# More Strassen pairs in the first layer, an accumulation seeded in PSUM, and a literal instruction order for groups 2 to 8

## Chip, cores, metric

One core of one Trainium2 chip. The metric is the device time of one execution in microseconds (us). Each time given is the median of several runs (3 to 11); all were in the fast state, so nothing has to be set aside as slow.

## The reference

Linear attention, whose output goes as tokens into a SwiGLU feed-forward block:

```
q_p, k_p = phi(q), phi(k)          # phi(x) = (x if x > 0 else exp(x) - 1) + 1; B=8, H=8, S=576, D=64
kv  = einsum('bhsd,bhse->bhde', k_p, v);   z = sum(k_p over s)
att = einsum('bhsd,bhde->bhse', q_p, kv) / (einsum('bhsd,bhd->bhs', q_p, z) + 1e-6)
x   = att as (4608 tokens, 512)
out = (silu(x @ w_gate) * (x @ w_val)) @ w_out      # hidden size 1536
```

The work goes in nine groups (0 to 8) of 512 tokens. For each group the kernel needs:

- the attention products. I call J the key-value products of one batch (72 small matmuls of 64x64 array tiles) and M the products that give a group's x (8 to 16 small matmuls);
- layer 1: gate and value products for twelve blocks of 128 hidden features. Plainly, a pair of blocks is sixteen matmuls with 512 columns; as one Strassen level it is seven products of four matmuls with 256 columns;
- layer 2: seven Strassen products for each of two token halves, 256 columns each. Both kernels have this from group 2 on.

TensorE makes the products, ScalarE the exponentials, silus, casts and part of the PSUM copies, VectorE the rest.

## The kernel before

The buffers of k, v, raw q and phi(q) were all double; batch b used half b % 2:

```
k16 = two([P, HL, J * D], FP16, "k16");  q16 = two(...);  v16 = two(...)
kp  = two([P, J, HL * D], FP16, "kp");   qp  = two(...);  vm  = two(...)

def load(src, dst, b):
    nc.gpsimd.dma_start(out=dst[b % 2][:, :, :], in_=heads(src, b))
```

A Strassen pair in layer 1 (only in the last two groups, `TS = (NG - 2, NG - 1)`, five pairs each): product 1 is copied to SBUF, product 2 is made in another bank, VectorE adds the two, ScalarE takes the silu.

```
def sp_keep(p, i, from_z, scale=1.0):
    nc.scalar.activation(out=sp_bufs(p)[0][i], in_=halves(sbanks[p % 3][from_z]), func=AF.Copy, bias=0.0, scale=scale)

def sp_gadd(p, th):
    (s, gg, _, _) = sp_bufs(p)
    nc.vector.tensor_tensor(out=gg[:, th, :, :], in0=halves(sbanks[p % 3][1]), in1=s[th], op=ALU.add)

def sp_silu(p, th):
    (_, gg, sl, _) = sp_bufs(p)
    nc.scalar.activation(out=sl[:, th, :, :], in_=gg[:, th, :, :], func=AF.Silu, bias=0.0, scale=1.0)
```

The group loop places the side work by hand, after a feature block of layer 1 or a product of layer 2. M and J stand side by side (cut):

```
for g in range(1, NG):
    b1, b2, b3 = g + 1, g + 2, g + 3
    ...
    for fb in range(FB if g in TS else 0, FB):
        l1(g, fb)
        for f in sl[fb]:
            f()
        if fb == 5 and b3 < B:
            ld_b(b3)                                              # k, q, v of a batch, in this order
    ...
    for (i, step) in enumerate(l2_steps(g)):
        ...
        if i == (7 if g in TS else 12 if b2 < B else 8) and b1 < NG:
            mm2(b1, (pV[1], pG[1], pV[0], pG[0]), "AVAV")         # M; x copies: ScalarE, VectorE in turn
        ...
        if i == 12 and b2 < B:
            joint(b2)                                             # J, its R copies and z diagonals
```

Of the kernel before, what the change touches and what calls it, by code (L numbers as in the profile page):

```python
# [13 lines left out]
P = 128  # L14
# [3 lines left out]
def kernel(  # L18
# [40 lines left out]
    prod = sb.tile([P, 4, HL * D], FP16, name="prod")  # L59
# [11 lines left out]
    xT = [two([P, U * C], FP16, f"xT{i}") for i in range(4)]  # L71
# [12 lines left out]
    id16 = sb.tile([P, P], FP16, name="id16")  # L84
    idx = sb.tile([P, P], mybir.dt.int32, name="idx")
# [7 lines left out]

    def load(src, dst, b):
        nc.gpsimd.dma_start(out=dst[b % 2][:, :, :], in_=heads(src, b))  # L95
# [22 lines left out]
    def exp_(src, e, b, lp):  # L118
        s = slice(2 * lp, 2 * lp + 2)
        nc.scalar.activation(out=e[:, s, :], in_=src[b % 2][:, s, :], func=AF.Exp, bias=0.0, scale=1.0)  # L120

    def plus_1(src, dst, b, lp):
        nc.vector.tensor_scalar(
            out=dst[b % 2][:, :, P * lp:P * lp + P].rearrange("p j (s d) -> p s j d", d=D),
            in0=src[b % 2][:, 2 * lp:2 * lp + 2, :].rearrange("p s (j d) -> p s j d", d=D), scalar1=0.0, scalar2=1.0,
            op0=ALU.max, op1=ALU.add)

    def least(e, dst, b, lp):
        d = dst[b % 2][:, :, P * lp:P * lp + P].rearrange("p j (s d) -> p s j d", d=D)
        nc.vector.tensor_tensor(out=d, in0=d, in1=e.rearrange("p s (j d) -> p s j d", d=D), op=ALU.min)  # L130
# [18 lines left out]
    def vcast(b, lp):  # L149
        s = slice(2 * lp, 2 * lp + 2)  # L150
        nc.scalar.activation(out=vm[b % 2][:, :, s, 0:D].rearrange("p j l d -> p l j d"),  # L151
                             in_=v16[b % 2][:, s, :].rearrange("p l (j d) -> p l j d", d=D),
                             func=AF.Copy, bias=0.0, scale=1.0)
# [4 lines left out]
    def terms_k(b, lp):  # L158

        return (kp[1], kp[0]) if b == 0 else (kp[b % 2],)  # L160

    def mm1(b, lp):
        if lp == 0:
            kvb[b] = ((pV[2], pX[0]), (pX[2], pV[2]), (pX[0], pX[1]), (pV[0], pG[0]), (pX[2], pV[2]))[min(b, 4)]
        for j in range(J):
            for (t, term_) in enumerate(terms_k(b, lp)):
                for hh in range(2):
# [7 lines left out]
                    for e in range(2):  # L175
# [4 lines left out]
                            rhs=v16[b][rows, 2 * lp + e, D * j:D * j + D] if b < 2 else vm[b % 2][rows, j, 2 * lp + e, :],  # L180
                            start=(j == 0), stop=(j == J - 1))

    def zdiag(b, lp):
        for hh in range(2):
            nc.vector.tensor_scalar(out=zd[:, 2 * hh + lp, :], in0=id16[:, :],
                                    scalar1=kvb[b][hh][:, 256 * lp + D:256 * lp + D + 1],
                                    scalar2=1.0 / SC, op0=ALU.mult, op1=ALU.mult)

    def r_copies(b):
        W = D  # L190
        for hh in range(2):
            nc.scalar.activation(out=R[b % 2][:, hh:4:2, 0:W],
                                 in_=kvb[b][hh][:, :].rearrange("p (i c) -> p i c", i=2)[:, :, 0:W], func=AF.Copy,
                                 bias=0.0, scale=1.0)
# [16 lines left out]
    def zb_copy(b):  # L211
        for hh in range(2):
            rows = slice(C * hh, C * hh + C)
            nc.scalar.activation(out=zbc[rows, :], in_=zps[b][rows, 256 * hh:256 * hh + 256], func=AF.Copy,
                                 bias=0.0, scale=1.0)
# [38 lines left out]
    def corners(ps, lhs, b, j0, j1, lps=(0, 1)):  # L254

        for lp in lps:
            for hh in range(2):
                for e in range(2):
                    rows = slice(D * e, D * e + D)
                    nc.tensor.matmul(out=ps[2 * lp + e][C * hh:C * hh + C, :], lhsT=lhs(2 * lp + hh, e),  # L260
                                     rhs=qT[b % 2][rows, j0:j1, lp, C * hh:C * hh + C], start=True, stop=True)

    def mm2(g, ps, engs):
        us = units(g)
        c00 = 2 * C if g == 2 else 0
        for b in sorted(set(u[0] for u in us)):
            js = [j for (bb, j) in us if bb == b]
            c0 = C * us.index((b, js[0]))
            if b > 1:
                corners([x[:, c0:c0 + C * len(js)] for x in ps], kv(b), b, js[0], js[-1] + 1)  # L270
        for i in range(4):
            dst = xT[i][g % 2][:, c00:]
            if engs[i] == "A":
                nc.scalar.activation(out=dst, in_=ps[i][:, c00:], func=AF.Copy, bias=0.0, scale=1.0 / SC)
            else:
                nc.vector.tensor_scalar(out=dst, in0=ps[i][:, c00:], scalar1=1.0 / SC, scalar2=None, op0=ALU.mult)  # L276
# [25 lines left out]
    TS = (NG - 2, NG - 1)  # L302
    HN = U * C // 2
    sbanks = ((pG[0], pV[0]), (pG[1], pV[1]), (pX[2], pV[2]))

    def flat(t):
        return t[:, :, :].rearrange("p a b -> p (a b)")

    wr = rr[:, :, :].rearrange("p a b -> p (a b)").bitcast(FP16)
    wl_all = ((wr[:, 0:10 * P], wr[:, 10 * P:20 * P]), (wl2[:, 0, :], wl2[:, 1, :]), (flat(k16[0]), flat(q16[0])),  # L310
              (flat(v16[0]), flat(kp[0])))

    def wl(m, c, f0, f1):
        return wl_all[m][c][:, P * f0:P * f1]

    def wl_sum(m, c, f0, f1):
        (g1, g2, v1, v2) = [w[:, i, P * f0:P * f1] for (w, i) in ((wg, c), (wg, 2 + c), (wv, c), (wv, 2 + c))]
        (a, b, op) = ((v1, v2, ALU.add), (wl(0, c, f0, f1), g1, ALU.subtract), (g1, v1, ALU.subtract),
                      (g2, wl(1, c, f0, f1), ALU.subtract))[m]
        nc.vector.tensor_tensor(out=wl(m, c, f0, f1), in0=a, in1=b, op=op)  # L320

    def x_blk(g, kh, th, c):
        return xT[2 * kh + c][g % 2][:, HN * th:HN * th + HN]

    def x_sum(g, m, c):
        (a, b) = ((x_blk(g, 0, 1, c), x_blk(g, 0, 0, c)), (x_blk(g, 1, 1, c), xs[:, 0, c, :]),
                  (x_blk(g, 1, 1, c), x_blk(g, 0, 1, c)), (x_blk(g, 1, 0, c), xs[:, 1, c, :]))[m]
        nc.vector.tensor_tensor(out=xs[:, m, c, :], in0=a, in1=b, op=ALU.subtract)

    def sp_prd(g, p, n):  # L330
        dst = sbanks[p % 3][1 if n in (2, 3, 5) else 0]
        for e in range(2):
            for c in range(2):
                fs = slice(P * (2 * p + e), P * (2 * p + e) + P)
                lhs = {1: wg[:, c, fs], 2: wg[:, 2 + c, fs], 4: wv[:, 2 + c, fs]}
                lhs = lhs[n] if n in lhs else wl({3: 3, 5: 0, 6: 1, 7: 2}[n], c, 2 * p + e, 2 * p + e + 1)
                rhs = {1: x_blk(g, 0, 0, c), 2: x_blk(g, 1, 0, c), 3: x_blk(g, 1, 1, c), 4: xs[:, 3, c, :],
                       5: xs[:, 0, c, :], 6: xs[:, 1, c, :], 7: xs[:, 2, c, :]}[n]
                nc.tensor.matmul(out=dst[:, HN * e:HN * e + HN], lhsT=lhs, rhs=rhs,  # L339
                                 start=(n in (1, 2, 5) and e == 0 and c == 0), stop=(c == 1), skip_group_check=True)  # L340
# [4 lines left out]
    def f32(t, n):  # L345
        return flat(t).bitcast(FP32)[:, 0:n]

    def sp_bufs(p):
        i = p % 2
        s12 = f32((k16, v16)[i][1], 4 * HN).rearrange("p (i e t) -> p i e t", i=2, e=2)  # L350
        s5 = f32(q16[1], 4 * HN)[:, 2 * HN * i:2 * HN * i + 2 * HN].rearrange("p (e t) -> p e t", e=2)
        gg = f32((kp[1], ek)[i], 4 * HN).rearrange("p (h e t) -> p h e t", h=2, e=2)
        sl = vm[i][:, :, :, :].rearrange("p j l d -> p (j l d)")[:, 0:4 * HN].rearrange("p (h e t) -> p h e t", h=2, e=2)
        v22 = flat(prod)[:, 2 * HN * i:2 * HN * i + 2 * HN].rearrange("p (e t) -> p e t", e=2)
        return (s12[:, 0, :, :], s12[:, 1, :, :], s5), gg, sl, v22

    def sp_keep(p, i, from_z, scale=1.0):
        nc.scalar.activation(out=sp_bufs(p)[0][i], in_=halves(sbanks[p % 3][from_z]), func=AF.Copy, bias=0.0, scale=scale)

    def sp_gadd(p, th):  # L360
        (s, gg, _, _) = sp_bufs(p)
        nc.vector.tensor_tensor(out=gg[:, th, :, :], in0=halves(sbanks[p % 3][1]), in1=s[th], op=ALU.add)

    def sp_silu(p, th):
        (_, gg, sl, _) = sp_bufs(p)
        nc.scalar.activation(out=sl[:, th, :, :], in_=gg[:, th, :, :], func=AF.Silu, bias=0.0, scale=1.0)  # L366

    def sp_v22(p):
        (s, _, _, v22) = sp_bufs(p)
        nc.vector.scalar_tensor_tensor(out=v22, in0=halves(sbanks[p % 3][0]), scalar=SC, in1=s[2], op0=ALU.mult, op1=ALU.add)  # L370

    def sp_h21(g, p):
        nc.vector.scalar_tensor_tensor(out=hT[g % 2][:, 2 * p:2 * p + 2, 0:HN], in0=halves(sbanks[p % 3][0]), scalar=SC,
                                       in1=sp_bufs(p)[2][:, 0, :, :], op0=ALU.mult, op1=ALU.mult)

    def sp_h22(g, p):
        (_, _, sl, v22) = sp_bufs(p)
        eng = nc.vector if p > NP - 3 else nc.gpsimd
# [619 lines left out]
```

## Time and profile before

| | before |
|---|---|
| median of 3 runs | 305.61 us (305.47 to 305.94) |
| TensorE start-to-start, 512 / 256 columns | 216 / 109 ns |
| from group 2's first matmul to the last matmul start | 84.86 to 298.42 us |

The first view is the page of the kernel before: its busy times, and TensorE's busy share in tenths in forty slices.

```profile
PE 295.6 (97%) x2596; PEld 181.0 (60%) x2596; DVE 247.6 (82%) x526; ACT 193.1 (64%) x313; POOL 49.2 (16%) x61
...
PE   7899999999999999999999999999999999999993
```

PE is TensorE, DVE is VectorE, ACT is ScalarE. TensorE is busy nearly always, but matmul records overlap, so "busy" does not say that the stream has no holes. Starts do. The second view is a piece of the chain of waits (start, length, instruction, count):

```profile
174.17 1.97 PE pX L502 x18
...
182.11 0.86 PE pV L287 x4
```

Eighteen 256-column matmuls take 1.97 us (109 ns each), four 512-column ones 0.86 us (216 ns each), one after another with nothing between. The third view is the table of windows: busy time (and instructions) of each engine in three stretches, which are groups 2, 3 to 5, and 6 to 8 roughly.

```profile
core 0: us, PE busy (x) PEld busy (x) DVE busy (x) ACT busy (x) POOL busy (x), PEclk, DMA share, GB/s
84.50:116.00 31.50, 31.50 (x270) 18.60 (x269) 25.90 (x54) 19.91 (x31) 2.23 (x3) 1.00 0.54 97
116.00:208.00 92.00, 92.00 (x710) 53.93 (x709) 83.72 (x178) 60.20 (x101) 3.70 (x5) 1.00 0.46 89
208.00:298.00 90.00, 90.00 (x784) 66.58 (x783) 76.75 (x166) 52.64 (x103) 6.91 (x6) 1.00 0.22 48
```

VectorE (third figure) is second: 83.72 of 92 us in groups 3 to 5. The fourth view is TensorE's timeline around M in group 6 (most of M's rows left out):

```profile
237.09 0.82 PE L502 MATMUL pX<-ws,hs 128*128 128x256 f16 x6
237.84 0.37 PE L260 MATMUL pV<-qT,R 64*64 64x448 f16 x1
...
238.40 0.83 PE L502 MATMUL pX<-ws,hs 128*128 128x256 f16 x6
```

### The profile page before, as it was taken

What the parts mean: (1) busy time and instruction counts of PE and PEld (TensorE: products, weight loads), DVE (VectorE), ACT (ScalarE), POOL (GpSimd) and SP (SyncE); (2) the same over time, 40 slices, a digit from 0 to 9 for tenths busy, and PEclk for the clock granted to TensorE, in tenths of its full rate; (3) what the DMA queues carried; (4) which work ended last, traced back from release to release, by engine and by line L of the source; (5) the groups of instructions that cost most, each with busy time, mean ns of one, the idle gap of its engine ahead of it and who ended that gap; (6) DMA issues with size and microseconds to landing.
All of it is one profiled execution on the core that took longest, in us unless ns stands there. A gap on an engine that the chain in (4) does not pass through costs nothing.

```text
span 303.4 us, 6676 instructions
## 1 busy us (share of the span) xinstructions
PE 295.6 (97%) x2596; PEld 181.0 (60%) x2596; DVE 247.6 (82%) x526; ACT 193.1 (64%) x313; POOL 49.2 (16%) x61
## 2 busy tenths in 40 slices
PE   7899999999999999999999999999999999999993
PEld 5644454444544485448644774477446888878882
DVE  4754649888859998998799889987999878968991
ACT  4864978858563698358846685568633478548931
POOL 8664256310010001000100000000000004001300
PEclk9999999999999999999999999999999999999998
DMA  8999999999979229911892132123312050033014
GB/s 214 193 196 201 206 208 220 199 212 191 133 147 154 51 31 201 190 34 29 173 197 56 28 81 62 34 46 71 71 26 54 22 119 0 2 74 67 2 37 104
DMA packets 41472, 32.88 MB, mean 108 GB/s; under 512 B 16400, under 2 KB 36816, under 8 KB 41440
## 3 DMA queue, kind: packets, MB, share of 16 engines
q0 software_dynamic: 20176, 18.35, 39.1%
q1 hardware_dynamic: 21104, 13.97, 20.1%
q8 instruction: 20, 0.33, 0.5%
q10 hardware_dynamic: 160, 0.13, 0.2%
q14 instruction: 12, 0.10, 0.1%
HBM read 37.75 MB, written 9.44 MB: 156 GB/s over the span
## 4 chain that ended last, share of the span: by engine, by line
PE 89%; issue 4%; DMA 2%; ACT 1%; DVE 1%; POOL 0%; POOLq 0%; DVEq 0%; ACTq 0%
PE pV L287 23%; PE pG L287 21%; PE pX L502 14%; PE pV L502 4%; PE pV L339 4%; PE pG L339 4%; PE pG L446 4%; PE pV L446 4%; PE pX L287 3%; DMA q<-in_q_dram 2%; PE pV L260 1%; PE pX L260 1%; PE pX L339 1%; PE pX L177 1%; PE pV L407 1%
## 5 line engine op out<-in xcount | busy, mean ns | idle before, releaser
L287 PE MATMUL pV<-xT,wv 128*128 128x512 f16 x324 | 83.5, 379 | 0.0
L287 PE MATMUL pG<-xT,wg 128*128 128x512 f16 x296 | 76.4, 379 | 0.0
L292 ACT ACTIVATE sil<-pG 128x512 f16<-128x512 f32 x74 | 43.5, 597 | 47.1 <-PE pG L287 32.2
L293 DVE SCALAR_TENSOR_TENSOR hT<-pV,sil 128x512 f16<-128x512 f32 x81 | 55.0, 686 | 15.0 <-PE pV L287 7.6
L287 PEld LDWEIGHTS <-wv 128*128 128x128 f16 x336 | 32.9, 98 | 39.7
L287 PEld LDWEIGHTS <-wg 128*128 128x128 f16 x336 | 32.3, 98 | 39.1 <-DVE xT L276 0.8
L502 PEld LDWEIGHTS <-hs 128*128 128x128 f16 x336 | 32.5, 98 | 4.7 <-DVE hs L476 0.4
L379 POOL TENSOR_TENSOR hT<-prod,vm 128x512 f16<-128x512 f16 x6 | 6.9, 1152 | 127.5 <-ACT vm L366 127.5
L502 PEld LDWEIGHTS <-hT 128*128 128x128 f16 x252 | 24.3, 98 | 4.1
L502 PE MATMUL pX<-ws,hs 128*128 128x256 f16 x210 | 25.7, 273 | 0.0
L507 ACT ACTIVATE part<-pX 128x256 f32<-128x256 f32 x35 | 12.8, 380 | 13.2 <-PE pX L502 13.2
L476 DVE TENSOR_TENSOR hs<-hT 128x512 f16<-128x512 f16 (+2 forms) x42 | 17.4, 418 | 0.2
L241 DVE TENSOR_TENSOR qp<-qp,rden 128x768 f16<-128x768 f16 x18 | 17.1, 948 | 0.0
L228 DVE TENSOR_REDUCE den<-prod 128x12 f32<-128x768 f16 x18 | 16.9, 942 | 0.0
L120 ACT ACTIVATE ek<-k 128x1152 f16<-128x1152 f16 x14 | 16.1, 1160 | 1.2 <-DMA k<-in_k_dram 1.1
L95 POOL DMA_DIRECT2D k<-in_k_dram x7 | 5.2, 745 | 64.1 <-ACT part L507 44.0
L502 PE MATMUL pX<-wo,hT 128*128 128x256 f16 x126 | 15.2, 273 | 0.0
L130 DVE TENSOR_TENSOR kp<-kp,ek 128x1152 f16<-128x1152 f16 x14 | 10.6, 758 | 5.4 <-ACT ek L120 5.0
L446 PEld LDWEIGHTS <-hT 128*128 128x128 f16 x96 | 8.7, 98 | 10.3 <-issue 0.8
L151 ACT ACTIVATE vm<-v 128x1152 f16<-128x1152 f16 x12 | 14.1, 1173 | 0.0
L120 ACT ACTIVATE eq<-q 128x1152 f16<-128x1152 f16 x12 | 13.3, 1169 | 0.0
L512 DVE SCALAR_TENSOR_TENSOR osb<-pX,part 128x256 f32<-128x256 f32 x28 | 11.0, 418 | 2.1 <-PE pX L502 1.9
(186 smaller groups left out, 513.7 us busy)
## 6 DMA issues: line engine op xcount, KB each, us to landing
out_dram<-osb SPq DMA_DIRECT2D x64, 128.0 KB, 3.0
k<-in_k_dram POOLq DMA_DIRECT2D x7, 576.0 KB, 8.8
q<-in_q_dram POOLq DMA_DIRECT2D x7, 576.0 KB, 11.4
v<-in_v_dram POOLq DMA_DIRECT2D x7, 576.0 KB, 13.5
wg<-in_moe_w_gate_dram POOLq DMA_DIRECT2D x5, 256.0 KB, 9.0
wv<-in_moe_w_val_dram POOLq DMA_DIRECT2D x5, 256.0 KB, 9.2
wo<-in_moe_w_out_dram POOLq DMA_DIRECT2D x2, 512.0 KB, 15.1
out_dram<-osb SPq DMA_DIRECT2D x13, 64.0 KB, 2.0
```

Of the source, the lines that this page charges most:

```text
L120: nc.scalar.activation(out=e[:, s, :], in_=src[b % 2][:, s, :], func=AF.Exp, bias=0.0, scale=1.0)
L151: nc.scalar.activation(out=vm[b % 2][:, :, s, 0:D].rearrange("p j l d -> p l j d"), in_=v16[b % 2][:, s, :].rearrange("p l (j d) -> p l j ...
L228: nc.vector.tensor_reduce(out=den[:, HL * j0:HL * j1], in_=prod[:, 0:j1 - j0, :].rearrange("p j (l d) -> p (j l) d", d=D), axis=AX.X, op=A ...
L241: nc.vector.tensor_tensor(out=qv, in0=qv, in1=rden[:, HL * j0:HL * j1].unsqueeze(2).to_broadcast([P, HL * (j1 - j0), D]), op=ALU.mult)
L287: nc.tensor.matmul(out=ps[:, :], lhsT=src[:, i, P * fb:P * fb + P], rhs=xT[i][g % 2][:, :], start=(i == 0), stop=(i == 3))
L292: nc.scalar.activation(out=s[:, :], in_=pg[:, :], func=AF.Silu, bias=0.0, scale=1.0)
L293: nc.vector.scalar_tensor_tensor(out=hT[g % 2][:, fb, :], in0=pv[:, :], scalar=SC, in1=s[:, :], op0=ALU.mult, op1=ALU.mult)
L339: nc.tensor.matmul(out=dst[:, HN * e:HN * e + HN], lhsT=lhs, rhs=rhs, start=(n in (1, 2, 5) and e == 0 and c == 0), stop=(c == 1), skip_gr ...
L446: nc.tensor.matmul(out=pso[(g, t)][:, :], lhsT=hT[g % 2][:, fb, P * t:P * t + P], rhs=wo[:, fb, :], start=(fb == 0), stop=(fb == FB - 1))
L476: (eng or nc.vector).tensor_tensor(out=o, in0=a, in1=b, op=op)
L502: nc.tensor.matmul(out=(z if n in (2, 3, 5) else x)[:, 0:HD], lhsT=left(f), rhs=right(f), start=(f == 0 and n in (1, 2, 5)), stop=(f == HF ...
L507: nc.scalar.activation(out=part[:, 2 * i + tt, :], in_=(x if from_x else z)[:, 0:HD], func=AF.Copy, bias=0.0, scale=1.0 / SC)
```

## The change

Its intent: fewer TensorE cycles. A Strassen pair trades 16 x 216 ns for 28 x 109 ns. Groups 3 to 5 get two pairs each and groups 6 to 8 six each (24 instead of 10). To pay for it elsewhere, product 1 is copied by ScalarE into the PSUM bank where product 2 then accumulates on it ("seeded"), so that VectorE need not add; the buffers of k, v and raw q become single from batch 3 on, which frees room for the weight sums; and groups 2 to 8 are recorded as 1181 operations and issued in a fixed, literal order. (Each operation is recorded with a duration that nothing else uses; that a search over these durations found the order is our reading of the code. "Searched order" below means this order.)

The core of the diff (long parts cut, marked):

```
+    def ix(b):
+        return b % 2 if b < 3 else 1
     def load(src, dst, b):
-        nc.gpsimd.dma_start(out=dst[b % 2][:, :, :], in_=heads(src, b))
+        nc.gpsimd.dma_start(out=dst[ix(b)][:, :, :], in_=heads(src, b))
@@ (same for k, v, raw q everywhere; phi(q) stays at b % 2; one fused x tile, wider x sums)
-    TS = (NG - 2, NG - 1)
+    NP = {2: 0, 3: 2, 4: 2, 5: 2, 6: 6, 7: 6, 8: 6}
@@ a pair's product n into bank dst; product 2 no longer starts its bank
-                                 start=(n in (1, 2, 5) and e == 0 and c == 0), stop=(c == 1), skip_group_check=True)
+                                 start=(n in (1, 5) and e == 0 and c == 0), stop=(c == 1), skip_group_check=True)
+        if n == 1:
+            op("ACT", 0.52, lambda: keep_1(bx, halves(by)), [nm(bx)], [nm(by)])        # the seed
+        if n == 2:
+            op("ACT", 0.52, lambda: silu_1(halves(by), sl0), [nm(by), "table"], [f"ek{i}.0"])
@@ x copies: three on ScalarE, one on VectorE
+    XE = {g: "AVAA" for g in range(NG)}
@@ layer 2: M apart from J, and in two halves M0, M1 in groups 6 and 7
+    ORDER = {g: "10 11 20 21 60 61 50 51 70 71 30 M 31 40 J 41" for g in (2, 3, 4)}
+    ORDER[5] = "10 11 20 21 60 61 50 51 70 71 M 30 31 | 40 41 J"
+    for g in (6, 7):
+        ORDER[g] = "10c 11c 20c 21c M0 10d 11d 20d 21d M1 60 61 50 51 70 71 30 | 31 40 41"
@@ (the recorded operations, cut)
+    steps = """
+        0 1 14 15 17 4 16 35 2 36 8 19 18 38 3 5 39 37 41 40 20 42 6 44 45 43 47 21 46 48 50 49 51 22 53 52 25
@@ (1181 numbers in all)
+    """
+    for i in steps.split():
+        ops[int(i)][2]()
```

## The prediction

> **What bounds the kernel now.** TensorE. The page gives PE 97% busy, but its records overlap, so I checked starts: in the chain of waits, four 128x512 matmuls take 0.86 us (216 ns each) and eighteen 128x256 matmuls 1.97 us (109 ns each). That is the spacing of a gapless stream in the Trainium skill, "TensorE: Matmul & The Clock Gate", section "Back-to-back issue gap" (N/2.4 + 2.5 ns: 215.8 and 109.2); this trace agrees with that formula, not with the sustained 131 ns for N=512 given there too. From 85 us (group 2) to the last matmul at 298.4 us, only about 1.3 us lies beyond that spacing: 0.09 us at each block of attention products, 0.05 to 0.1 us at group boundaries, 0.3 us in the last group. The granted clock is 1.00. In the table of windows a steady group takes 31.5 us, groups 7 and 8 28.6 us. VectorE comes second: 28.5 of 31.5 us busy in groups 3 to 5; ScalarE 20.7.
>
> **What the change does to TensorE.** Groups 0 and 1 are unchanged. A Strassen pair in layer 1 replaces sixteen 128x512 matmuls (16 x 216 = 3.46 us) by twenty-eight 128x256 (28 x 109 = 3.05 us): 0.40 us saved. Groups 7 and 8 had 5 pairs each; now groups 3 to 5 have 2 each and groups 6 to 8 six each: 24 instead of 10. The instruction listing confirms it: 224 fewer 128x512 and 392 more 128x256 matmuls, all else equal; -48.4 + 42.7 = -5.65 us, all on the critical path. The fixed order can win little, as there were hardly any gaps: at most 0.5 us (boundaries; layer 2 products of the last groups now start inside layer 1).
>
> **What it costs elsewhere.** By VectorE's start-to-start times in this trace (0.60 us for a 512-wide PSUM operation, 0.33 for a 512-wide fp16 sum, 0.47 for 768-wide), a pair costs VectorE 2.13 us instead of 1.2; x sums (1.3 us a group) and weight sums (16, 7.5 us in groups 2 to 5) come on top; wider hidden sums and one x copy moved to ScalarE give some back. My sums: 28.5 to 31 us of VectorE work a group in groups 2 to 5 against 27 to 28 before, while TensorE's own time falls to about 30.7 us in groups 3 to 5 and 28 in 6 to 8. VectorE is then at 93 to 98%: a second limit right under the first. Seeding in PSUM removes one VectorE addition per pair. Single k, v and raw q buffers from batch 3 on make loads start later; they had 9 to 13 us to landing, which fits a 30 us group.
>
> **Prediction.** 305.6 - 5.65 = 300.0; minus up to 0.5 us of gaps, plus 0.3 to 2 us of new small TensorE waits on VectorE: 300.2 us, range 299.3 to 302.0. Chances: faster by over 2% (below 299.5) 0.20, within 2% 0.79, slower 0.01.
>
> **What would show it.** Windows: groups 0 and 1 equal; group 2 about 31.4 us, 3 to 5 about 30.7, 6 about 28, 7 and 8 about 28.2. Layer 1 matmuls still 216 and 109 ns apart. VectorE near 30 us busy in groups 2 to 5. Any PE wait over 0.1 us released by VectorE is the new loss.
>
> **What would make it wrong.** Faster: gaps I count as inherent vanish. Slower: VectorE falls behind in groups 2 to 4, delaying PSUM banks; a load landing late into the single buffers stops the in-order VectorE or ScalarE; the fixed order proves fragile on the chip.

## More of the kernel before

```profile
L151 ACT ACTIVATE vm<-v 128x1152 f16<-128x1152 f16 x12 | 14.1, 1173 | 0.0
```

The six products from 237.09 end their share of the stream at 237.09 + 6 x 0.109 = 237.74; M starts at 237.84, so 0.10 us is lost on the way from 128x128 to 64x64 array tiles. ScalarE never waited for a v load.

## The result

| | before | after |
|---|---|---|
| median | 305.61 us (305.47 to 305.94, 4 runs) | 303.05 us (302.71 to 303.95, 4 runs) |
| ratio, 95% interval | | 0.9919 (0.9897 to 0.9942) |

Ratios here and below are the mean time of one kernel's runs over that of the other's of the same rounds, so not quite the ratio of the medians. The class is "same" (within 2%). The kernel got 2.6 us faster, where 5.4 had been predicted, and the median lies 1.05 us above the upper end of the range.

The page and the windows of the kernel after:

```profile
PE 292.4 (97%) x2764; PEld 197.2 (65%) x2764; DVE 256.8 (85%) x531; ACT 217.3 (72%) x361; POOL 42.3 (14%) x55
...
PE   7899999999999999999999999999999999999993
```

```profile
84.50:116.00 31.50, 31.50 (x267) 18.22 (x265) 30.43 (x59) 21.23 (x34) 3.16 (x5) 1.00 0.57 88
116.00:208.00 92.00, 91.52 (x814) 61.17 (x801) 88.52 (x183) 70.88 (x121) 4.98 (x7) 1.00 0.59 108
208.00:298.00 90.00, 87.78 (x870) 76.23 (x868) 77.47 (x161) 65.03 (x128) 0.56 (x1) 1.00 0.26 56
```

VectorE is at 96 to 97% in the first two stretches, as predicted. TensorE now has unbusy time: 0.48 us in the middle stretch. ScalarE took the most new work, 10.7 us there.

To see what is beyond the arithmetic I went through every TensorE start from group 2's first matmul to the last. A full-array matmul is allowed N/2.4 + 2.5 ns (215.8 and 109.2 ns, the spacing that both traces show); whatever its successor comes later is a gap. Gaps before a block of small products are kept apart, and the small products are simply measured. All in us:

| | full-array matmuls at that spacing | small products | gaps before small blocks (number) | other gaps | sum |
|---|---|---|---|---|---|
| before | 206.23 | 5.97 | 0.56 (6) | 0.79 | 213.56 |
| after | 200.68 | 6.68 | 1.71 (12) | 1.97 | 211.04 |
| change | -5.55 | +0.71 | +1.15 | +1.18 | -2.52 |

So the saving came in full: 512-column matmuls fell from 517 to 293, 256-column ones rose from 867 to 1259, at unchanged spacing. And 3.04 us of it was lost again inside the same stretch. (Group 2 starts at 84.86 us before and 85.14 after, which is within what its start varies by among the later runs, 84.9 to 85.7. The end after the last matmul start is 5.0 us in both.)

Read from first layer-1 matmul to first layer-1 matmul, group 2 took 31.6 us (31.4 predicted), group 3 31.9 (30.7 predicted) and group 4 31.1 (30.7 predicted); before, each took 31.5. Group 3 is where most is missing.

Three places hold nearly all of the loss.

*Place 1: a late load in group 3.* The chain of waits from 110 to 150 us, which was all TensorE before, now passes through DMA:

```profile
115.05 0.74 POOL q L100
115.79 13.86 DMA v<-in_v_dram
129.70 1.06 issue
```

And this is ScalarE's timeline there; brackets hold the idle time before an instruction and what ended it:

```profile
126.69 0.60 ACT L361 ACTIVATE rr<-pX 128x512 f32<-128x512 f32 x1
129.68 1.19 ACT L156 ACTIVATE vm<-v 128x1152 f16<-128x1152 f16 x1 [2.39 <-DMA v<-in_v_dram]
130.76 0.57 ACT L364 ACTIVATE ek<-pV 128x512 f16<-128x512 f32 x1
131.23 0.59 ACT L364 ACTIVATE sil<-pG 128x512 f16<-128x512 f32 x1
```

ScalarE stands 2.39 us before the cast of v. Two silus stand behind it in its order; their banks are what TensorE needs next, and VectorE's chain is delayed as well. TensorE's gaps over the next 20 us: 0.19 us at 131.5, 0.34 at 133.4, 0.04 at 136, 0.33 at 139, 0.2 within J at 147, 0.28 at 149. For the one at 139 the timeline names VectorE, in words that will matter later:

```profile
139.60 0.28 PE L440 MATMUL pX<-wo,hT 128*128 128x256 f16 x1 [0.16 <-DVE hT L370]
```

*Place 2: a table load at 210 us.* ScalarE, then TensorE:

```profile
209.34 0.58 ACT L361 ACTIVATE pV<-pG 128x512 f32<-128x512 f32 x1 [0.66 <-PE pG L347]
209.94 1.28 ACT L947 ACT_TABLE_LOAD   x1
211.23 0.66 ACT L445 ACTIVATE osb<-pX 128x256 f32<-128x256 f32 x2
```

```profile
210.87 0.27 PE L347 MATMUL pG<-xs,q 128*128 128x256 f16 x1
211.66 0.22 PE L182 MATMUL pX<-vm,kp 64*64 64x65 f16 x2 [0.52 <-ACT osb L445]
```

J writes the bank that the output copy reads, and the copy stands behind the table load: 211.66 - 210.87 - 0.109 = 0.68 us of gap.

*Place 3: twelve blocks of small products instead of six.* Where M was one block in group 6, it is two blocks of halves (and likewise in group 7):

```profile
231.76 0.27 PE L440 MATMUL pV<-wo,hT 128*128 128x256 f16 x1
231.97 0.41 PE L264 MATMUL pG<-qT,R 64*64 64x448 f16 x8
232.31 0.50 PE L440 MATMUL pX<-wo,hT 128*128 128x256 f16 x3
232.65 0.27 PE L440 MATMUL pV<-wo,hT 128*128 128x256 f16 x1
232.85 0.41 PE L264 MATMUL pV<-qT,R 64*64 64x448 f16 x8
233.20 1.26 PE L440 MATMUL pX<-ws,hs 128*128 128x256 f16 x10
```

Each half pays about 0.09 us to get in (231.76 + 0.109 = 231.87, start at 231.97) and runs 0.34 to 0.35 us to the next full-array matmul. So M in halves costs 2 x (0.09 + 0.345) = 0.88 us, where M whole cost 0.10 + 0.56 = 0.66. In groups 2 to 5, where M and J were adjacent, they are now apart: 0.56 + 0.71 us and one more entrance, against 0.46 + 0.74 together; 0.165 us a group. Four times 0.165 and twice 0.22 is 1.1 us. The Trainium skill, "TensorEngine Tiling (Array Packing)", section "Key Properties", says that changing the tiling mode drains the TensorE. The trace agrees in that every change of array tile shows a gap (that the gap is the drain is not shown separately). Going in costs 0.09 us. Coming out costs about 0.09 us, by an estimate: in the kernel before, the last 512-column product of M starts at 266.69 us and the next full-array one 0.308 us later, where 512 columns are otherwise spaced by 0.216.

### The profile page after: what moved, and what is told of

It is laid out like the page before. It is cut to its first block, busy times and chain, and to the rows that moved or that the text cites. A ratio compares the mean times of both kernels' runs of the same rounds, so it can differ in the third digit from the quotient of the medians.

```text
span 301.2 us, 6998 instructions
## 1 busy us (share of the span) xinstructions
PE 292.4 (97%) x2764; PEld 197.2 (65%) x2764; DVE 256.8 (85%) x531; ACT 217.3 (72%) x361; POOL 42.3 (14%) x55
## 4 chain that ended last, share of the span: by engine, by line
PE 43%; issue 41%; DMA 7%; DVE 3%; ACT 3%; POOL 1%; POOLq 0%; ACTq 0%; DVEq 0%
DMA v<-in_v_dram 7%; PE pV L293 6%; PE pV L866 6%; PE pG L866 5%; PE pG L293 4%; PE pX L440 4%; PE pX L293 4%; PE pG L379 4%; PE pV L379 4%; PE pX L347 2%; PE pX L264 1%; PE pV L440 1%; ACT eq L125 1%; DVE hs L409 1%; DVE hT L370 1%
## 5 line engine op out<-in xcount | busy, mean ns | idle before, releaser
L866 PE MATMUL pV<-xt,wv 128*128 128x512 f16 x144 | 38.9, 379 | 0.0
L866 PE MATMUL pG<-xt,wg 128*128 128x512 f16 x144 | 38.4, 379 | 0.2 <-ACT sil L364 0.2
L364 ACT ACTIVATE sil<-pG 128x512 f16<-128x512 f32 x36 | 21.4, 597 | 20.0 <-PE pG L866 16.3
L440 PEld LDWEIGHTS <-hT 128*128 128x128 f16 x252 | 24.1, 98 | 5.0 <-DVE hT L370 0.4
L370 DVE SCALAR_TENSOR_TENSOR hT<-pV,sil 128x512 f16<-128x512 f32 x36 | 24.7, 686 | 2.0 <-ACT sil L364 1.3
L866 PEld LDWEIGHTS <-wv 128*128 128x128 f16 x144 | 14.1, 98 | 12.6 <-issue 0.6
L299 DVE SCALAR_TENSOR_TENSOR hT<-pV,sil 128x512 f16<-128x512 f32 x21 | 14.2, 690 | 9.3 <-ACT sil L298 5.2
L293 PE MATMUL pV<-xt,wv 128*128 128x512 f16 x84 | 21.9, 379 | 0.0
L364 ACT ACTIVATE ek<-eq 128x512 f16<-128x512 f32 x24 | 15.0, 627 | 6.5 <-DVE eq L895 6.4
L440 PE MATMUL pX<-wo,hT 128*128 128x256 f16 x126 | 17.1, 273 | 0.2 <-DVE hT L370 0.2
L347 PE MATMUL pV<-xt,wg 128*128 128x256 f16 x120 | 17.0, 273 | 0.0
L293 PEld LDWEIGHTS <-wv 128*128 128x128 f16 x96 | 9.4, 98 | 11.3
```

The lines of the kernel that those rows point to most:

```text
L293: nc.tensor.matmul(out=ps[:, :], lhsT=src[:, i, P * fb:P * fb + P], rhs=xT[i][g % 2][:, :], start=(i == 0), stop=(i == 3))
L299: nc.vector.scalar_tensor_tensor(out=hT[g % 2][:, fb, :], in0=pv[:, :], scalar=SC, in1=s[:, :], op0=ALU.mult, op1=ALU.mult)
L347: nc.tensor.matmul(out=dst[:, HN * e:HN * e + HN], lhsT=lhs, rhs=rhs, start=(n in (1, 5) and e == 0 and c == 0), stop=(c == 1), skip_group ...
L364: nc.scalar.activation(out=dst, in_=src, func=AF.Silu, bias=0.0, scale=1.0)
L370: nc.vector.scalar_tensor_tensor(out=hT[g % 2][:, fb, :], in0=pv[:, :], scalar=SC, in1=s[:, :], op0=ALU.mult, op1=ALU.mult)
L440: nc.tensor.matmul(out=(z if n in (2, 3, 5) else x)[:, 0:HD], lhsT=left(f), rhs=right(f), start=(i == 0 and fs[0] == 0 and (n in (1, 5) or ...
```

## The experiments

Theory 1: the lost 3 us is made of single waits, caused by the order of things: ScalarE standing before one DMA and one table load, and TensorE's changes of tile mode. Theory 2, the one in the prediction: VectorE at 96% is a second limit, and gaps are its way of showing.

Most kernels move single operations of the fixed order. The edit is always of this form, inserted before the operations are issued; (x, y) puts operation x right after operation y:

```
+    seq = [int(i) for i in steps.split()]
+    for (x, y) in MOVES:
+        seq.remove(x)
+        seq.insert(seq.index(y) + 1, x)
```

Results were correct except where said. Medians; the kernel before was 305.60, 305.48 and 305.45 us in the three batches of runs.

| run | what | median us (range) | ratio to before | gap and small-product time, us |
|---|---|---|---|---|
| a0_again | the change, unaltered | 303.43 (302.46 to 303.57) | 0.9923 | 10.89 |
| e1_v_early | v loads earlier | 302.09 (301.37 to 302.26) | 0.9884 | 9.17 |
| e2_table_early | table load earlier | 302.75 (302.29 to 303.80) | 0.9917 | 9.92 |
| e3_both | both | 301.39 (301.35 to 301.40) | 0.9865 | 8.82 |
| e4_whole_m | e3, M whole in 6 and 7 | 301.03 (301.00 to 301.23) | 0.9853 | 8.67 |
| e5_zd_tail | e3, other orders at four places | 301.52 (301.19 to 301.96) | 0.9864 | 8.85 |
| e6_dve_light | e3, VectorE relieved (wrong result) | 301.46 (301.31 to 301.53) | 0.9865 | 8.68 |
| e9_all | e3 + e4 + e5 | 301.28 (301.02 to 302.07) | 0.9864 | 8.71 |
| e7_no_seed | e3, no seeding in 6 to 8 | 312.26 (311.99 to 312.51) | 1.0224 | 19.68 |
| e8_as_recorded | the change without its order | 412.31 (410.75 to 414.04) | 1.3501 | |
| e10_zd4 | e4, one copy moved | 300.91 (300.78 to 301.85) | 0.9862 | 8.47 |
| e11_m_by_j | e10, M beside J in 2 to 4 | 302.94 (302.53 to 303.28) | 0.9918 | 10.46 |

The last column is what the ledger holds beside full-array matmuls: small products, gaps before them and other gaps (before 7.32, after 10.36). It comes from one trace of each kernel.

Medians alone cannot decide the small differences here. In the traces of the ledger group 2 starts anywhere from 84.86 to 85.66 us, although groups 0 and 1 have the same code in all runs of the changed kernel; most of this arises in the first 40 us, from a cause that was not looked for, and it is passed on to the end in full. It is in every median and every range; the ledger, which begins with group 2, is free of it.

### a0_again: the change again

No edit.

> The changed kernel once more, unaltered, as the yardstick for the others of this call. Expected by every theory: 303.0 us, 302.5 to 303.6, ratio to before 0.990 to 0.993; in the profile the same TensorE gaps: some 0.5 us at 131 to 134 us, 0.3 at 139, 0.3 at 149, 0.7 at 211.

It reproduces: 303.43 us. In its profile ScalarE's wait for v was longer (2.9 us) and the gap at 131.4 us was 0.72 instead of 0.19; in the first profile of the kernel after it was 2.39 us. By the ledger the two traces differ by 0.53 us (10.36 and 10.89), which is that gap. The landing of this one load thus moves a run by half a microsecond; the start of group 2 moves it too.

### e1_v_early: v loads right after the buffer is free

```
MOVES = ((126, 12), (300, 178), (474, 353))     # three v loads, after the casts of the batch before
```

> The loads of v for batches 5 to 7 are moved ahead in the order, to just after the casts that free their buffer; nothing else moves. Theory 1 (late load): in group 3 ScalarE waits 2.4 us for v (issued at 115.8, landed at 129.7 us), and being in order it holds back the silus and then VectorE, which costs about 1.2 us of TensorE gaps between 131 and 150 us. It expects ScalarE's wait gone, those gaps under 0.3 us, and 1.0 to 1.4 us less than a0_again, about 301.8 us. Theory 2 (VectorE, at 93 to 98% of these groups, is the second limit, and the gaps are its backlog): at most 0.4 us less.

1.34 us faster than a0_again by medians, 1.72 us by the ledger. The v loads in groups 2 to 3 of both kernels: the first fence is the kernel after, the second e1, and then ScalarE in e1 where it had stood for 2.39 us.

```profile
DMA to landing us min/median/max: 13.9/13.9/13.9
```

```profile
DMA to landing us min/median/max: 5.7/6.2/6.7
```

```profile
126.50 1.30 ACT L361 ACTIVATE rr<-pX 128x512 f32<-128x512 f32 x2
127.70 1.18 ACT L156 ACTIVATE vm<-v 128x1152 f16<-128x1152 f16 x1
```

The load now leaves at 102.7 us instead of 115.79, and lands in less than half the time, with no k and q load beside it. There is no wait before the cast, and TensorE's gaps from 131 to 139 us are gone, that at 149 shrank from 0.28 to 0.19. VectorE's work is the same as before the edit. In the kernel after, the load was late for a reason of order: the three loads stand in one queue as k, q, v, the buffers are single, k and q must wait for the exponentials of the batch before, and v stood behind them though its own buffer had been free since about 102 us. Size of place 1 by the ledger: 10.36 - 9.17 = 1.19 us against the kernel after. The Trainium skill, "DMA: Bandwidth & Descriptors", section "Anatomy of one DMA — SWDGE (gpsimd) path", gives 2.0 us plus bytes / 436e3 for one load; for the 576 KB of this one I estimate 3.35 us from it. Measured: 5.7 to 6.7 us nearly alone, 13.9 as the third of three issued within 2.6 us. The measurement decides: it is not a figure to plan a load by here.

### e2_table_early: the table load in ScalarE's idle time

```
MOVES = ((644, 668),)     # the load of the silu table, before product 1's seed instead of after
```

> In group 5 the activation table load (1.28 us on ScalarE) is moved ahead of two products' copies, to just after the x copies, where ScalarE idled 0.66 us. Theory 1 (the table load stands between the last product of layer 2 and the copy that frees its PSUM bank for the next key-value product): the 0.69 us TensorE gap at 211 us falls under 0.15 us, and the time by 0.5 to 0.7 us against a0_again. Theory 2 (VectorE backlog): the gap gets another releaser, VectorE, and at most 0.2 us is won.

ScalarE and TensorE in e2:

```profile
208.39 1.28 ACT L947 ACT_TABLE_LOAD   x1
209.69 0.58 ACT L361 ACTIVATE pV<-pG 128x512 f32<-128x512 f32 x1
210.44 0.66 ACT L445 ACTIVATE osb<-pX 128x256 f32<-128x256 f32 x2 [0.18 <-PE pX L440]
```

```profile
210.64 0.27 PE L347 MATMUL pG<-xs,q 128*128 128x256 f16 x1
210.88 0.22 PE L182 MATMUL pX<-vm,kp 64*64 64x65 f16 x2
```

The gap before J fell from 0.68 to 0.13 us; 0.08 us appeared before a pair's product just ahead of it, and that before the next zb (the small matmul that spreads the denominators) grew from 0.07 to 0.19. By medians it is worth 0.68 us, but six runs from 302.29 to 303.80 make that inconclusive. The ledger falls by 0.44 us against the kernel after, 0.07 of it in the gaps of place 1.

### e3_both: both

```
MOVES = ((126, 12), (300, 178), (474, 353), (644, 668))
```

> Both edits together. Theory 1: the gains add, 1.6 to 2.0 us less than a0_again, about 301.2 us, ratio to before 0.985 to 0.987. Theory 2: at most 0.6 us less.

301.39 us: the two gains add (by medians 2.04 us together, 1.34 and 0.68 singly). In the ledger it is 2.07 us against a0_again, of which the table load is only 0.35 (e1 to e3). The four runs lie within 0.05 us, but that is no proof that the late load made the time vary: e1, e9 and e10, where it is gone too, spread over 0.9 to 1.1 us.

### e4_whole_m: two changes of tile mode fewer

```
MOVES = (...e3..., (825, 834), (981, 990))     # M0 to where M1 is, in groups 6 and 7
```

> On top of e3_both: in groups 6 and 7 the first half of the x products is moved back to just before the second half, so that TensorE changes from full-array to 64x64 products and back once instead of twice. Theory 1 (each such change costs about 0.2 us that the order's fixed durations do not contain: two halves took 0.35 + 0.35 us and 0.09 + 0.1 us around each, against 0.56 to 0.57 us in one block in the kernel before): 0.3 to 0.5 us less than e3_both, about 301.0 us, ratio to before 0.985. Rival (the halves cost the same in one block, and their place matters more): no gain or a loss, because the x copies start 0.4 us later.

0.36 us faster than e3 by medians of two batches (0.9853 against 0.9865), but between the two traces (301.35 and 301.01 us) 0.24 us is an earlier start of group 2. In the ledger the small products fell by 0.25 us and the gaps before them by 0.19, while a layer 2 product that now comes earlier waits 0.15 us for its hidden block in each of the two groups: 0.15 us net. So place 3 is as costly as counted, and two thirds of its price in groups 6 and 7 had bought something.

### e5_zd_tail and e9_all: other small orders

```
MOVES = (...e3..., (343, 344), (698, 697), (694, 695), (1127, 1125))
# z diagonals (zd) ahead of the copies of R from the same PSUM bank, recorded with J in groups 3 and 5; one hidden sum of group 8 earlier
```

> On top of e3_both: in groups 4 and 6 VectorE's zd operations are placed ahead of ScalarE's R copies of the same PSUM bank, and in group 8 one hidden sum is moved ahead of the last hT product. Theory 1 (these are waits in a chain of short operations, not load): the two gaps of about 0.2 us before the zb product (at 148 and 212 us) fall under 0.05 us, the gap of 0.31 us at 287.6 falls to about 0.1 us; together 0.4 to 0.6 us less than e3_both, about 300.9 us. Rival (VectorE backlog): the zb gaps stay above 0.15 us each.

A miss: 301.52 us, and the ledger is that of e3 (8.85 against 8.82). The gap before zb at 148 us is gone, but in group 6 there are new ones of 0.08 and 0.31 us, and the gap of 0.31 us between the layers in group 8 did not move.

> All edits of e3_both, e4_whole_m and e5_zd_tail together. Theory 1: 0.7 to 1.1 us less than e3_both, 300.3 to 300.7 us, ratio to before 0.983 to 0.984, so faster than the kernel before and the changed one; what is left above 300.0 us is the changes between full-array and small products and 0.3 us in group 8. Rival: no better than e3_both by more than 0.3 us.

A miss too: 301.28 us, with e5's new gaps (ledger 8.71, where e4 alone had 8.67). Of the three places that e5 touched, one gained (148 us), one lost (group 6) and one did not move (group 8): in an order this tight, moving an instruction can open a gap behind as well as close one ahead.

### e6_dve_light: is VectorE's load the limit?

```
-  in_=prod[...].rearrange("p j (l d) -> p (j l) d", d=D),
+  in_=prod[...].rearrange("p j (l d) -> p (j l) d", d=D)[:, :, 0:D // 2],        # denominators from half the columns
@@ the same for the scaling of phi(q): half the columns. e3's MOVES. Wrong on purpose (relative error 26).
```

> On top of e3_both, wrong on purpose: VectorE's sums and scalings of the denominators read and write only half of the columns, which takes 2.5 us of work from VectorE in every group from 1 to 7 and leaves every instruction and every wait in place. Theory 1 (TensorE is bound by its own work plus a few chained waits; VectorE is full but not late): at most 0.4 us less than e3_both, 301.0 to 301.4 us. Theory 2 (VectorE at 93 to 98% is the second limit): 1 us less or more, 300.4 us or below.

The windows of the middle stretch: e3 first, then e6.

```profile
116.00:208.00 92.00, 91.97 (x820) 62.25 (x810) 89.86 (x186) 71.99 (x123) 4.44 (x6) 1.00 0.57 102
```

```profile
116.00:208.00 92.00, 91.97 (x856) 62.29 (x844) 84.43 (x187) 71.91 (x124) 4.44 (x6) 1.00 0.58 101
```

VectorE has 5.4 us less to do there (1.8 us a group, not the 2.5 expected), and the time is 301.46 against 301.39 us; both ratios are 0.9865. In the ledger 0.14 us is won, all at one gap before zb at 212 us. Theory 2, which asked for 1 us, falls: at 98% busy VectorE is not what TensorE waits for in e3.

### e7_no_seed: what the seed is worth

```
@@ groups 6 to 8, e3's MOVES: product 1 is kept in SBUF, product 2 starts its own bank
-            op("ACT", 0.52, lambda: keep_1(bx, halves(by)), [nm(bx)], [nm(by)])
+            op("ACT", 0.52, lambda: keep_1(bx, s1t), [nm(bx)], [nm(by)])
@@ and before the silu of product 2
+                    nc.vector.tensor_tensor(out=s1t, in0=halves(by), in1=s1t, op=ALU.add)
```

> On top of e3_both: in groups 6 to 8 the first output of a pair is no longer seeded in PSUM; ScalarE copies product 1 to SBUF and VectorE adds it to product 2 (0.60 us more of VectorE a pair, 3.6 us a group, plus one more step in the chain before the silu). By my sums VectorE's work in these groups rises from 26.3, 24.6 and 22.6 us to about 30, 28 and 26 us against 28 us of TensorE. Expected if VectorE becomes the limit where its sum passes TensorE's: 2 to 4 us more than e3_both, 303.4 to 305.4 us. If instead only waits in chains matter and VectorE has room: under 1 us more.

Much slower than any theory had it: 312.26 us, 10.9 us above e3's median (of another batch) for 18 pairs, 0.6 us a pair. The view of waits from 208 to 310 us (engine and line, what it waited for; us, times, longest):

```profile
ACT ek L364 <- DVE sil L894: 16.5, 18, 1.4
...
PE pV L347 <- ACT sil L361: 3.8, 6, 0.9
...
PE pG L347 <- ACT sil L361: 3.3, 8, 0.8
```

In each of the 18 pairs ScalarE, in its fixed order, waits for VectorE's sum (16.5 us in all), and TensorE then waits for a bank that ScalarE has not copied. VectorE itself is not full: 86.4 of 100 us. The seed is worth more by the step that it takes out of the chain TensorE, ScalarE, VectorE, ScalarE than by VectorE's time. That is for this order; one that knew of the added step might lose less, which was not tried.

### e8_as_recorded: without the searched order

```
-    for i in steps.split():
-        ops[int(i)][2]()
+    for o in ops:
+        o[2]()
```

> The changed kernel with the operations of groups 2 to 8 issued in the order in which they are recorded, without the searched order: same work, same buffers. If the searched order is what makes the work fit, VectorE's and ScalarE's blocks of attention work (recorded in one piece) hold up the PSUM banks of layer 1: 12 to 40 us more, 315 to 345 us. Rival (TensorE is bound by its own work, the order hardly matters): under 306 us.

The same operations take 412.31 us, further off than expected. TensorE is busy 78%, and part of the loss is its clock (mean 0.911). Its timeline at the first long wait, and then the windows in that wait and behind it (the last but two figure is the granted clock):

```profile
87.91 1.03 PE L866 MATMUL pV<-xt,wv 128*128 128x512 f16 x4
100.47 1.87 PE L866 MATMUL pG<-xt,wg 128*128 128x512 f16 x4 [11.54 <-ACT sil L364]
```

```profile
98.00:100.00 2.00, 0.00 (x0) 0.00 (x0) 0.00 (x0) 2.00 (x3) 0.00 (x0) 0.50 0.00 0
100.40:104.40 4.00, 3.93 (x10) 1.45 (x10) 3.15 (x6) 1.26 (x4) 0.00 (x0) 0.51 0.02 4
```

After 11.5 us without work matmuls of 512 columns start 427 ns apart for about 4 us. This agrees with the Trainium skill, "TensorE: Matmul & The Clock Gate", section "Part 1: The HAM clock gate (the "warmup" mystery)": half rate after an idle window of about 3.4 us. The shorter waits of the other kernels, up to 1.5 us, left the spacing at 216 and 109 ns. So the prediction's "the fixed order can win little" was wrong as a statement about the order: without it, in the order of recording, the new work does not fit at all. (It says nothing of how a good hand order would do, nor of how the old work would run if recorded this way.)

### e10_zd4 and e11_m_by_j: a better version, and why M and J stand apart

```
e10: MOVES = (...e4..., (343, 344))     # the one of e5's moves that had helped
e11: MOVES = (...e10..., (150, 162), (151, 150), (324, 336), (326, 293), (498, 510), (502, 498), (500, 508))   # M next to J, groups 2 to 4
```

> e4_whole_m plus the one half of e5_zd_tail that worked in its trace (in group 4 VectorE's zd ahead of ScalarE's R copy): the gap of 0.19 us before the zb product at 148 us goes, 0.1 to 0.3 us less than e4_whole_m, 300.7 to 300.9 us, ratio to before about 0.9843. If the gap reappears elsewhere, as in group 6 of e5_zd_tail: 301.0 us.

300.91 us: the best median of all, a little under e4's 301.03, and within its spread. It beats both kernels (ratio to before 0.9862, 0.9841 to 0.9884), still within 2%. Its ledger has 8.47 us of gaps and small products, 0.20 less than e4's: the gap before zb at 148 us is gone and no new one came.

> e10_zd4 plus: in groups 2 to 4 the x products are moved back to just before the key-value products, so that TensorE leaves the full-array products once a group and not twice, as in the kernel before. Theory 1 (each change costs about 0.2 us): 0.1 us of each pair of changes is lost again to a wait for x at the group boundary (0.05 to 0.1 us in the kernel before), so 0.3 to 0.5 us less than e10_zd4, 300.3 to 300.6 us. Rival (the early x products pay for themselves): equal or slower, 300.8 to 301.5 us, with TensorE waiting for x copies at the boundaries.

With M next to J the small products of groups 3 and 4 fell to 0.46 + 0.72 us as before the change (in group 2 they kept their 1.27) and three entrances went, 0.47 us in all; but new waits came, and net 2.0 us were lost: 0.19 and 0.49 us at 118, 0.25 at 148 and 1.46 before zb at 180 us. The two longest run through ScalarE's order. At 180 us its x copies, now later, end at 179.44; behind them stands a table load of 1.28 us (179.46), and only behind that the copy of R (180.75) for which VectorE's last z diagonal waits, and zb with it. At 118 us the output copy that frees TensorE's bank stands behind the table load in the same way. So in this order 0.165 us a group for having x early was cheap, and part of place 3 is a price, not a fault. Whether M beside J would pay with the table load moved as in e2 was not tried.

## Why the prediction was wrong

- **TensorE's arithmetic, -5.65 us on the critical path: right.** The ledger shows -5.55 (it allows 215.8 and 109.2 ns where the sum used 216 and 109). Spacing, counts and clock were as said, groups 0 and 1 unchanged.
- **"Minus up to 0.5 us of gaps": right in size.** The small gaps at the ends of the plain groups' layer 2 (0.05 to 0.1 us each, 0.33 in all) are gone.
- **The step that failed: "plus 0.3 to 2 us of new small TensorE waits on VectorE".** With 300.2 as its middle, the prediction left +0.25 us for all that is not arithmetic; it was +3.04 in the ledger. The runs put in its place: late v load 1.19 us (after against e1), changes of tile mode 1.1 (counted; of the 0.44 that e4 took away 0.15 came back net), the table load 0.56 in the gap before J, of which 0.35 came back net when moved (e1 against e3); the remaining 0.2 is a sum of small ones with both signs, such as +0.3 between the layers of group 8 and the -0.33 above.
- **Its cause failed too: "VectorE is then at 93 to 98%: a second limit right under the first".** The load was right (96% in the middle stretch), the conclusion not: in e3, where the load is 98%, taking away 5.4 us of it won 0.14 us in the ledger and nothing in the median (e6). The test that the prediction named, waits "released by VectorE", would have misled as well: the gap at 139 us was released by VectorE's product, and went away when a DMA was moved (e1).
- **"They had 9 to 13 us to landing, which fits a 30 us group" failed.** It compared the wrong spans. A single buffer shortens the time between the release by one batch and the use by the next; of the 27.0 us from 102.7, when e1 shows the buffer free, to the landing at 129.65, 13.1 passed before the load left behind k and q, and 13.9 until it landed. 2.4 us sooner would have done. The prediction did name "a load landing late into the single buffers" as a risk, in the right engine, but gave it no time.
- **No term for changes of tile mode.** The prediction read "0.09 us at each block of attention products" from the profile and did not count the blocks after: twelve instead of six. The listing of operations would have told.
- **"Seeding in PSUM removes one VectorE addition per pair": right, and too small a view** (e7: 0.6 us a pair in this order, through the chain).

That the time did stay within 2%, as forecast, owes nothing to the cause that was named; the arithmetic put it there.

Open: the two gaps between the layers of group 8 (0.15 and 0.31 us in the kernel after, and the same in e1 to e6 and e9 to e11), which e5 failed to move; why group 2 starts up to 0.8 us later in some runs; and whether a new search with true durations of loads would beat 300.9 us.

## What to carry to other kernels

When one engine's stream is full, cost a change by that engine's arithmetic and then look for single waits: where an in-order engine stands before a DMA or a table load with someone else's work behind it, and how often TensorE changes its tile mode. A high busy share on a second engine is not yet a limit; take some of its work away and see if the time moves. Judge gains of a few tenths of a microsecond in the stretch that was changed, since the start of a run can vary by more. When buffers go from two to one, reckon for each load when it can leave (its buffer and the loads ahead in its queue) and when it is needed.

## What the Trainium skill lacked or had wrong

- "TensorEngine Tiling (Array Packing)" says that a mode change drains TensorE but gives no time: here 0.09 us from 128x128 to 64x64 and, by the estimate above, about 0.09 us back.
- "TensorE: Matmul & The Clock Gate", section "Back-to-back issue gap", calls 131 ns the sustained spacing for 512 columns and 216 the isolated one; here streams of weight load and matmul ran at 216 ns throughout (109 for 256 columns), before and after. It is that section which differs from the trace, not the whole page.
- "ScalarE: Activation LUTs", section "What ACT_TABLE_LOAD costs", adds about 1.38 us of drain to the load of 1.28 us. In both places shown here the next instruction started 1.29 to 1.30 us after the load did (209.94 to 211.23, 208.39 to 209.69), and the load 0.02 us after the end of the instruction before it; no such drain is seen.
- "DMA: Bandwidth & Descriptors": the formula for one load gives an estimated 3.35 us for 576 KB; here 5.7 to 6.7 us nearly alone and 13.9 us as the third of three issued within 2.6 us. No figure there tells what loads in one queue do to each other.
